# An attention-and-MLP block: another order of work for the first group of 512 rows

## The chip, the cores and the metric

The kernel runs on one core of a Trainium2 chip. The metric is the device time of one execution in microseconds (us), lower is better. A core has TensorE (PE, with its weight loads shown apart as PEld), VectorE (DVE), ScalarE (ACT), GpSimd (POOL) and SyncE (SP), which here issues nearly all transfers. Each engine works through its own instructions in order.

## The reference

```python
mod = (silu(c) @ w_mod)                       # c: 1x448, w_mod: 448x2688 -> six rows of 448
sa, ca, ga, sb, cb, gb = six rows of mod
h = layernorm(x) * (1 + ca) + sa              # x: 2048 x 448
q, k, v = split(h @ wqkv)                     # 16 heads of 28
scores = q @ k.T * 28 ** -0.5                 # key at most 255 rows back, causal
x = x + ga * ((softmax(scores) @ v) @ wo)
h = layernorm(x) * (1 + cb) + sb
x = x + gb * (mish(h @ w1 + b1) @ w2)         # w1: 448x1792, w2: 1792x448
```

All of it is float32. The kernel reaches that precision with two-part numbers: a value is split into `hi` (rounded to fp32r) and `lo` (the rest), and a product is the sum of `hi*hi`, `hi*lo` and `lo*hi`.

## The kernel before, in words

The 2048 rows are worked through in four groups (`NG`) of 512 (`GT`). For each group the normalised rows are transposed in four chunks `ci` of 128 features (the last one holds 64 features twice, for `hi` and `lo`), scaled and shifted by the modulation columns `cols`, and split into `hh` and `hl`. Then `wqkv` is applied in eleven matmuls a tile (`passes`). The tiles 0 to 6 hold 128 columns each of q and k: 0 to 3 reach over q, and 3 (its second half) to 6 over k. The tiles `v0` to `v3` hold V for 128 rows each.

q and k go out through `qk_out`: ACT copies `hi`, DVE forms `lo`, and `put` stores both to a scratch tensor `scr` in HBM. `L(i)` loads head i's q and k back from there, with features and parts on 84 partitions. The function waits on SP until the stores that it reads have landed.

For a head i, `A(i, t)` multiplies q and k for 128 rows, and DVE takes the maxima of the rows (line 580); `M2` transposes the maxima of two heads and sends them by DMA into rows 84 and 85 of the q tile, so that `B(u)` gets the scores with the maxima already subtracted. ACT takes the exponential twice (`P` and `Ph`), POOL forms the rest `Pl`, and `PV` multiplies both with V. `A` runs `LEAD` = 3 heads ahead of `B`.

Between these steps PE gets other work from generators. `fill_main(g)` yields the projections that are still missing, then the transposes and projections of the next group; a credit that grows by `RATE[g]` per step says how many. `fill_side(g)` yields small jobs: the norm of the next group, the modulation of `wo` and others. `pipe` delays the copies behind a tile by a step each, and `later` holds transfers that are issued one at a time or all at once by `flush`. `need(keys, g)` flushes and runs fillers until the given tiles are stored; `load_slot(i)` calls it and then `L(i)`.

The first group has an order of its own, written out by hand (lines 365 to 406):

- SP issues `cT`, x of group 0 (two pieces), the four pieces of `w_mod`, twenty of `wqkv`, then x of group 1.
- DVE takes the statistics of the four row tiles, then sums `w_mod` weighted by `sT` into `acc01` (`mod_sum`, line 145 and 147).
- POOL takes one reciprocal root for all four tiles (lines 206, 207) and the negated mean (211, 212); ACT normalises tile by tile (218).
- PE transposes each tile (376) and then multiplies `acc01` with ones, one column at a time (`mod_cols`, 152), so that the modulation stands on partitions; `mod_cols_out` copies it to `cols`.
- ACT forms `hh` (239), DVE `y` in place (236) and `hl` (243).
- ACT and POOL split the first 384 columns of the weights, ACT, DVE and POOL the other two blocks (164, 170, 172).
- PE does the tiles 0, 3 and 4 together in three rounds (`first`, line 401); all three are then copied and stored.
- POOL builds the mask, `fdf`, the constant columns of V and the rows of -1 in the six K tiles (lines 412 to 433).
- Fillers run until all V tiles are done; five heads are loaded; then `A` runs for three heads with fillers between.

Of the kernel before, what the change touches and what calls it, by code (L numbers as in the profile page):

```python
# [18 lines left out]
EPS = 1e-5  # L19
# [32 lines left out]
def adaln_block(ctx: ExitStack, tc: tile.TileContext, x, wqkv, wo, w1, b1, w2, c, w_mod, out):  # L52
# [19 lines left out]
    vp, vp_s = pool("vp")  # L72
    st0, st0_s = pool("st0")
# [3 lines left out]

    ACT.add_instruction(mybir.InstLoadActFuncSet(
# [18 lines left out]
    cT = cst.tile([112, 4], F32, name="cT")  # L97
# [35 lines left out]
    cols = cst.tile([128, 4, 4], F32, name="cols")  # L133

# [63 lines left out]
    def gen_ln(tiles, pl, xn_tiles, key, act=False, mv=None):  # L198
# [10 lines left out]
        if act:  # L209
            nm = pl.tile([128, 4], F32, name=f"nm{key}")  # L210
            POOL.tensor_tensor(nm, mv[:, :, 0], rs, op=ALU.mult)
            POOL.tensor_scalar(nm, nm, -1.0, None, op0=ALU.mult)
        yield
        xs = xn_tiles()
        for t in range(4):
            xn = xs[t]
            if act:
                ACT.activation(xn[:, 0:D], tiles[t], AF.Identity, scale=rs[:, t:t + 1], bias=nm[:, t:t + 1])
# [8 lines left out]
        if not act:  # L227
            dup(xs[3])
# [12 lines left out]
    def hT_lo(p, ci, hh, hl, si):  # L241
        hT_y(p, ci, si)
        DVE.tensor_tensor(hl[:, ci], p, hh[:, ci].bitcast(F32), op=ALU.subtract)
# [9 lines left out]
    def gen_ln1(g, act=False):  # L253
        def xn_tiles():
            return [xin[g][:, t] for t in range(4)]
        for r in gen_ln([xin[g][:, t, 0:D] for t in range(4)], qk, xn_tiles, f"a{g}", act):
            if r:
                XS[g] = r
            yield "dve"
# [42 lines left out]
    later = []  # L302

# [4 lines left out]
    def qk_out(g, m, p, st=None):  # L308
        st = st or qk.tile([128, 2, GT], F32R, name=f"st{g}_{m}", tag="qs", bufs=3)
# [11 lines left out]

        def put():
            for a, b, pa, ph in ((0, qn, 0, 2), (qn, 128, 1, 0)):
                if a < b:
                    dma(scr[r0 + a:r0 + b, pa:pa + 2, gs], st[a:b].bitcast(F32))
                    dma(scr[r0 + a:r0 + b, ph, gs], st[a:b, 0].bitcast(F32))
# [39 lines left out]
    ln0 = gen_ln1(0, True)  # L366
    for _ in range(5):
        next(ln0)
    for k in range(4):
        mod_sum(k, wm01[k], acc01)  # L370
    pm = bank("sA", 2, "mc01")
    trs = [bank(("sB", "mm")[ci // 2], 2, f"tr0{ci}") for ci in range(4)]
    for t in range(4):
        next(ln0)
        for ci in range(4):
            PE.transpose(trs[ci][:, t * 128:(t + 1) * 128], XS[0][t][:, ci * 128:(ci + 1) * 128], ident)
# [13 lines left out]
    x_load(1)  # L390
    for c0, c1 in QCOLS[1:]:
        for ci in range(4):
            split_hi(wqs[ci][:, c0:c1], wq3[:, ci, c0:c1], ACT)
    for (c0, c1), eng in zip(QCOLS[1:], (DVE, POOL)):
        for ci in range(4):
            split_lo(wqs[ci][:, c0:c1], wq3[:, ci, c0:c1], wql[:, min(ci, 2), c0:c1], ci, eng)
    first = [(m, bank(tag, b, f"qk0_{m}"), qk_passes(0, m)) for m, tag, b in ((0, "pv", 1), (3, "tr", 1), (4, "sA", 2))]
    for lo_n, hi_n in ((0, 3), (3, 6), (6, 11)):
        for m, p, ps in first:
            for n in range(lo_n, hi_n):  # L400
                PE.matmul(p, ps[n][1], ps[n][0], start=(n == 0), stop=(n == 10))
    for m, p, ps in first:
        st = st0.tile([128, 2, GT], F32R, name="st0_4") if m == 4 else None
        for f in qk_out(0, m, p, st):
            f()
        flush()
    st0_s.close()
    att, att_s = pool("att")

    identr = att.tile([128, 128], BF16, name="identr")  # L410
    mask = att.tile([128, 384], F32, name="mask")
    POOL.memset(mask, 0.0)
    POOL.affine_select(mask, mask, pattern=[[1, 384]], compare_op=ALU.is_ge, fill=NEG, base=-1,
                       channel_multiplier=-1)
    POOL.affine_select(mask, mask, pattern=[[-1, 384]], compare_op=ALU.is_ge, fill=NEG, base=W,
                       channel_multiplier=1)
    fdf = att.tile([128, 512], F32, name="fdf", tag="P", bufs=3)
# [4 lines left out]
                       fill=-2.0 ** 100, base=0, channel_multiplier=-1)  # L422
    fdmask = att.tile([128, 256], BF16, name="fdmask")
    for v in V:
        POOL.memset(v[:, :, 28:29].bitcast(F32), 1.0)
        POOL.memset(v[:, :, 29:32].bitcast(F32), 0.0)
    Q2 = [att.tile([86, 2, GT], F32R, name=f"q2_{i}") for i in range(NQ // 2)]
    Q3 = [Q2[i // 2][:, i % 2] for i in range(NQ)]
    K3 = []
    for i in range(NK):  # L430
        t = att.tile([86, GT + W], F32R, name=f"k3_{i}")
        POOL.memset(t[64:86, :].bitcast(F32), -1.0)
        K3.append(t)
# [404 lines left out]
    def fill_main(g):  # L838
        if g == 0:
            yield from gen_qkv(0, VT + (1, 5, 2, 6))  # L840
# [34 lines left out]
    RATE = {0: 0.48, 1: 0.91, 2: 0.91, 3: 0.65}  # L875
# [8 lines left out]
    def need(keys, g):  # L884
        flush()
# [184 lines left out]
```

## Time and profile before

| | us |
|---|---|
| median of 3 runs | 734.92 (732.76 to 738.67) |
| profiled execution | 735.41 |
| its span, first to last instruction | 733.6 |
| PE busy | 692.8 (94%) |
| ACT, DVE, POOL busy | 392.0, 383.1, 326.5 |
| DMA | 83.86 MB, 114 GB/s over the span |

In the rows below a time is a microsecond of the span. In a row of the order of time, the first number is the start and the second the length; `x4` is a count, and the bracket tells how long the engine had been idle and what ended that. A line number is that of the kernel before.

### The profile page before, as it was taken

How to read it: one execution, taken by the hardware profiler on the slowest of the kernel's cores; microseconds unless marked ns; L12 is line 12 of the kernel's file. 1: busy time of each engine (PE TensorE's matmuls, PEld its weight loads, DVE VectorE, ACT ScalarE, POOL GpSimd, SP SyncE). 2: the span in 40 equal slices, each digit the busy share in tenths (PEclk: the TensorE clock that was granted, in tenths of full speed). 3: DMA queues.
4: the chain of work that ended last, by engine and by line, in shares of the span. 5: the costliest groups of instructions: out<-in, count | busy, mean ns of one | idle time of the engine just before them, and what ended most of it. 6: DMA issues, size and time to landing. Idle time of an engine off the chain costs nothing.

```text
span 733.6 us, 11903 instructions
## 1 busy us (share of the span) xinstructions
PE 692.8 (94%) x3969; PEld 589.6 (80%) x3969; DVE 383.1 (52%) x1014; ACT 392.0 (53%) x740; POOL 326.5 (45%) x358
## 2 busy tenths in 40 slices
PE   3987989999999999999999899999999999999996
PEld 3765767888889888888887678878888888888885
DVE  4858645587865688665667943342324132413113
ACT  3516767776776677767878974343223223322221
POOL 4624788676766586766778953523010000000000
PEclk9999999999999999999999999999999999999999
DMA  8675554365384364462566174400200020001001
GB/s 213 185 249 190 179 158 140 92 204 157 95 263 134 97 205 136 146 197 75 170 206 195 46 239 141 137 13 1 101 0 1 1 100 1 1 0 51 1 0 51
DMA packets 48121, 83.86 MB, mean 114 GB/s; under 512 B 6126, under 2 KB 26108, under 8 KB 48060
## 3 DMA queue, kind: packets, MB, share of 16 engines
q1 hardware_dynamic: 48060, 83.10, 37.5%
q8 instruction: 32, 0.52, 0.3%
q14 instruction: 29, 0.24, 0.1%
HBM read 53.45 MB, written 29.36 MB: 113 GB/s over the span
## 4 chain that ended last, share of the span: by engine, by line
PE 75%; DVE 9%; DMA 6%; ACT 4%; SPq 2%; issue 2%; POOL 1%; DVEq 0%; POOLq 0%; ACTq 0%
PE z L814 20%; PE pv L640 8%; PE qk L294 7%; PE acc L992 6%; PE acc L993 6%; PE acc L991 6%; PE sA L578 5%; PE wo L294 4%; PE sB L608 4%; PE qk_v L294 3%; PE sB L619 3%; DVE junk L580 3%; SPq L59 2%; PE et L651 1%; ACT P L622 1%
## 5 line engine op out<-in xcount | busy, mean ns | idle before, releaser
L630 POOL TENSOR_TENSOR Pl<-P,Ph 128x512 fp32r<-128x512 f32 (+2 forms) x192 | 232.9, 1221 | 84.4 <-ACT Ph L623 50.9
L580 DVE CUSTOM_DVE_ANT_0 junk<-sA,mask 128x384 f32<-128x384 f32 (+2 forms) x256 | 135.3, 529 | 105.2 <-PE sA L578 99.8
L622 ACT ACTIVATE P<-sB 128x512 f32<-128x512 f32 (+2 forms) x192 | 109.8, 572 | 67.7 <-PE sB L619 62.2
L822 DVE TENSOR_TENSOR al<-t,ah 128x512 fp32r<-128x512 f32 x56 | 38.8, 692 | 205.1 <-ACT ah L821 205.1
L820 ACT ACTIVATE t<-z,b1c 128x512 f32<-128x512 f32 x56 | 38.6, 689 | 193.2 <-PE z L814 182.2
L578 PE MATMUL sA<-k,q 84*128 84x384 f32 (+2 forms) x256 | 100.8, 397 | 9.7 <-DVE mx L580 5.4
L623 ACT ACTIVATE Ph<-sB 128x512 fp32r<-128x512 f32 (+2 forms) x192 | 109.3, 569 | 0.0
L814 PE MATMUL z<-hhf,w 128*128 128x512 f32 x224 | 89.4, 399 | 0.0
L814 PE MATMUL z<-hlf,w 128*128 128x512 f32 x224 | 88.8, 396 | 0.0
L991 PE MATMUL acc<-w2h,ah 128*128 128x448 f32 x224 | 82.2, 367 | 0.0
L992 PE MATMUL acc<-w2l,ah 128*128 128x448 f32 x224 | 82.0, 366 | 0.0
L993 PE MATMUL acc<-w2h,al 128*128 128x448 f32 x224 | 81.9, 366 | 0.0
L640 PE MATMUL pv<-Ph,v 128*60 128x256 f32 (+2 forms) x352 | 76.8, 292 | 2.2 <-ACT o L645 2.1
L640 PE MATMUL pv<-Pl,v 128*60 128x256 f32 (+2 forms) x352 | 74.1, 285 | 3.1 <-POOL Pl L630 3.0
L608 PE MATMUL sB<-q,k 86*128 86x256 f32 (+1 forms) x352 | 74.7, 286 | 1.3 <-DMA q<-mr 1.2
L814 PE MATMUL z<-hhf,w1l 128*128 128x512 f32 x168 | 66.3, 395 | 0.0
L608 PEld LDWEIGHTS sB<-q,k 86*128 86x128 f32 x352 | 61.7, 190 | 3.3 <-DMA q<-mr 1.5
L578 PEld LDWEIGHTS sA<-k,q 84*128 84x128 f32 x256 | 49.0, 193 | 18.0 <-DVE mx L580 11.5
L619 PE MATMUL sB<-fdmask,identr 128*128 128x128 bf16 (+1 forms) x320 | 60.3, 254 | 0.0
L640 PEld LDWEIGHTS pv<-Ph,v 128*60 128x60 f32 x352 | 45.6, 133 | 16.6 <-ACT o L645 4.3
L640 PEld LDWEIGHTS pv<-Pl,v 128*60 128x60 f32 x352 | 45.0, 132 | 13.2 <-POOL Pl L630 6.3
L645 ACT ACTIVATE o<-pv 60x512 f32<-60x512 f32 x64 | 37.8, 591 | 24.0 <-PE pv L640 23.2
(149 smaller groups left out, 1257.9 us busy)
## 6 DMA issues: line engine op xcount, KB each, us to landing
scr<-st SPq DMA_DIRECT2D x24, 512.0 KB
k<-scr SPq DMA_DIRECT2D x48, 252.0 KB
q<-scr SPq DMA_DIRECT2D x64, 168.0 KB
scr<-st SPq DMA_DIRECT2D x32, 256.0 KB
x<-x1d SPq DMA_DIRECT2D x10, 448.0 KB
xin<-in_A_x_dram SPq DMA_DIRECT2D x8, 448.0 KB
xr<-in_A_x_dram SPq DMA_DIRECT2D x16, 224.0 KB
x1d<-xr SPq DMA_DIRECT2D x16, 224.0 KB
```

The lines of the kernel that those rows point to most:

```text
L294: PE.matmul(p, b, a, start=(n == 0), stop=(n == 10))
L578: PE.matmul(p[:, c0:384], q[0:84, t * 128:(t + 1) * 128], k[0:84, t * 128 + c0:t * 128 + 384], start=True, stop=True)
L580: DVE.tensor_tensor_reduce(out=junk[:, c0:384], in0=p[:, c0:384], in1=mask[:, c0:384], scale=1.0, scalar=-3.0e38, op0=ALU.add, op1=ALU.max ...
L608: PE.matmul(p[:, c:c + 128 * (t1 - t0)], k[:, jj * 128:(jj + 1) * 128], q[:, t0 * 128:t1 * 128], start=(n == 0), stop=False, skip_group_ch ...
L622: ACT.activation(P[:, c0:], p[:, c0:], AF.Exp, scale=SCALE)
L623: ACT.activation(Ph[u][:, c0:], p[:, c0:], AF.Exp, scale=SCALE)
L630: eng.tensor_tensor(Pl[u][:, a:b], Pt[u][:, a:b], Ph[u][:, a:b].bitcast(F32), op=ALU.subtract)
L640: PE.matmul(pv[0:60, t0 * 128:t1 * 128], V[j % NV][:, h, :], P[u][:, c:c + 128 * (t1 - t0)], start=(P is Ph and b == 0 and n == 0), stop=F ...
L814: PE.matmul(zb[n], ps[m][1], ps[m][0], start=(m == 0), stop=(m == 10))
L991: PE.matmul(p, ah[n][:, ts], w2h[f], start=(f == 0), stop=False)
L992: PE.matmul(p, ah[n][:, ts], w2l[f], start=False, stop=False)
L993: PE.matmul(p, al[n][:, ts], w2h[f], start=False, stop=(f == NF - 1))
```

## The change

- `cT` is loaded through ACT's queue, ahead of ACT's table load. The last piece of `w_mod` comes in two transfers and is summed in two halves.
- The first norm takes its reciprocal roots for two tiles at a time; the negated mean is one DVE operation for two tiles.
- Dummy transposes of the identity (`warm`) stand on PE: 46 before the first real one, 2 after each row tile (4 after the last), 12 after the modulation columns.
- ACT forms `y` for the odd chunks in place of DVE. The weight splits of chunks 2 and 3 stand between the `hh`.
- POOL fills five of the six K tiles and the mask at the start; the V constants and `fdf` follow the first weight splits.
- PE does the tiles 0 and 3 first. Their stores that heads 0 and 1 need go out first, then L(0) and L(1), then the rest; then tile 4. The V block's weights are split by DVE (two) and POOL (two), the third block's likewise.
- After L(2) and L(3), nine filler steps run (v0, v1, tile 1), then `A` for three heads with a filler step after each of the twelve (before: one step after every second); L(4) follows the second head. Tile 6 is left for the main loop.
- In the main loop `RATE[0]` is 0.56 in place of 0.48, side steps of group 0 start two steps earlier, and `need` returns at once, without a flush, when its tiles are out.
- All fillers of group 0 take their PSUM banks from the tag `mm`.

```diff
+    cT = cst.tile([112, 4], F32, name="cT")
+    nc.scalar.dma_start(cT, c.rearrange("o (k p) -> p (o k)", p=112))
     ACT.add_instruction(mybir.InstLoadActFuncSet(
...
-    dma(cT, c.rearrange("o (k p) -> p (o k)", p=112))
     x_load(0)
...
-        dma(t, w_mod[k * 112:(k + 1) * 112, 0:2 * D])
+        for s in (slice(0, 2 * D),) if k < 3 else (slice(0, D), slice(D, 2 * D)):
+            dma(t[:, s], w_mod[k * 112:(k + 1) * 112, s])
...
+    def k3_tile(pl, i):
+        t = pl.tile([86, GT + W], F32R, name=f"k3_{i}")
+        POOL.memset(t[64:86, :].bitcast(F32), -1.0)
+        K3.append(t)
+    for i in range(NK - 1):
+        k3_tile(kq, i)
+    mask = kq.tile([128, 384], F32, name="mask")
...
+    for t in range(4):
+        ln_stats(xs0[t][:, 0:D], mv0[:, t, :], qk, f"a0{t}")
+        if t % 2:
+            h = slice(t - 1, t + 1)
+            POOL.tensor_scalar(rs0[:, 0, h], mv0[:, h, 1], EPS, None, op0=ALU.add)
+            POOL.tensor_tensor(rs0[:, 0, h], rs0[:, 0, h], mhalf[:, h], op=ALU.pow)
+    def nm0(t):
+        h = slice(t, t + 2)
+        DVE.scalar_tensor_tensor(rs0[:, 1, h], mv0[:, h, 0], -1.0, rs0[:, 0, h], op0=ALU.mult, op1=ALU.mult)
...
+    for k in range(3):
+        if k < 2:
+            nm0(2 * k)
         mod_sum(k, wm01[k], acc01)
+    for s in (slice(0, D), slice(D, 2 * D)):
+        mod_sum(3, wm01[3][:, s], acc01[:, s])
+    def warm(n):
+        for _ in range(n):
+            PE.transpose(wb[:, 0:128], ident, ident)
+    warm(46)
...
     for t in range(4):
-        next(ln0)
+        norm0(t)
         for ci in range(4):
             PE.transpose(trs[ci][:, t * 128:(t + 1) * 128], XS[0][t][:, ci * 128:(ci + 1) * 128], ident)
+        warm(2 + 2 * (t == 3))
     for i in range(2):
         mod_cols(acc01[:, i * D:(i + 1) * D], pm[:, 4 * i:4 * i + 4])
+    warm(12)
...
+    first_split(0)
+    first_split(1)
...
     for ci in range(4):
         hT_hi(trs[ci], ci, hh, 0)
-        hT_lo(trs[ci], ci, hh, hl, 0)
+        if ci % 2:
+            first_split(2 + ci // 2)
+            ACT.activation(trs[ci], trs[ci], AF.Identity, scale=cols[:, 1, ci:ci + 1], bias=cols[:, 0, ci:ci + 1])
+        hT_lo(trs[ci], ci, hh, hl, 0, ci % 2 == 0)
...
+    x_load(1)
+    split_cols(*QCOLS[1], (DVE, DVE, None, None))
+    first_tiles([(0, bank("pv", 1, "qk0_0")), (3, bank("tr", 1, "qk0_3"))])
+    for m in (0, 3):
+        PARTS[0, m].pop(0)()
+    PARTS[0, 0].pop(0)()
+    L(0)
+    L(1)
+    flush()
+    split_cols(*QCOLS[1], (None, None, POOL, POOL))
+    first_tiles([(4, bank("sA", 2, "qk0_4"))])
+    flush()
+    split_cols(*QCOLS[2], (POOL, POOL, DVE, DVE))
     st0_s.close()
...
-            yield from gen_qkv(0, VT + (1, 5, 2, 6))
+            yield from gen_qkv(0, VT[:2] + (1,) + VT[2:] + (5, 2, 6))
...
-    RATE = {0: 0.48, 1: 0.91, 2: 0.91, 3: 0.65}
+    RATE = {0: 0.56, 1: 0.91, 2: 0.91, 3: 0.65}
...
     def need(keys, g):
+        if all((g, m) in done for m in keys):
+            return
         flush()
...
-    for i in range(LEAD + 1):
+    for i in range(2, LEAD + 1):
         load_slot(i)
-    need({f"v{t}" for t in range(4)}, 0)
-    load_slot(LEAD + 1)
+    for _ in range(9):
+        fill0()
...
     for i in range(LEAD):
         for t in range(4):
             A(i, t)
-            if t % 2:
-                pipe.step()
-                next(fillers[0])
-                flush()
+            fill0()
             side_step(0, False)
         if i % 2:
-            pipe.step()
-            next(fillers[0])
             M2(i // 2)
+            load_slot(LEAD + 1)
...
-            if v > 1:
+            if v > 1 or g == 0:
                 side_step(g, k == 1 and a < NS)
```

More of the change, by code (lines that the diff above doesn't have):

```diff
@@ L226, in gen_ln @@
             yield xs
-        if not act:
-            dup(xs[3])
+        dup(xs[3])
     def tr_chunk(xs, ci, p):
@@ L251, in adaln_block, with gen_ln1 @@
     XS, HT = {}, {}
-    def gen_ln1(g, act=False):
+    def gen_ln1(g):
         def xn_tiles():
             return [xin[g][:, t] for t in range(4)]
-        for r in gen_ln([xin[g][:, t, 0:D] for t in range(4)], qk, xn_tiles, f"a{g}", act):
+        for r in gen_ln([xin[g][:, t, 0:D] for t in range(4)], qk, xn_tiles, f"a{g}"):
             if r:
@@ L320, in store, with rows @@
             later.append(put)
+        def rows(a, b, pa, ph):
+            if a < b:
+                dma(scr[r0 + a:r0 + b, pa:pa + 2, gs], st[a:b].bitcast(F32))
+                dma(scr[r0 + a:r0 + b, ph, gs], st[a:b, 0].bitcast(F32))
+        parts = [lambda: rows(qn, 128, 1, 0), lambda: rows(0, qn, 0, 2)]
         def put():
[L323 to L326, printed above, removed]
+            while parts:
+                parts.pop(0)()
             done.add((g, m))
+        PARTS[g, m] = parts
         return hi, lo, store
@@ L388, in adaln_block @@
         hT_hi(trs[ci], ci, hh, 0)
-        hT_lo(trs[ci], ci, hh, hl, 0)
[L390 to L405, printed above, removed]
-        flush()
[L407 to L417, printed above, removed]
+        if ci % 2:
+            first_split(2 + ci // 2)
+            ACT.activation(trs[ci], trs[ci], AF.Identity, scale=cols[:, 1, ci:ci + 1], bias=cols[:, 0, ci:ci + 1])
+        hT_lo(trs[ci], ci, hh, hl, 0, ci % 2 == 0)
+    for v in V:
+        POOL.memset(v[:, :, 28:29].bitcast(F32), 1.0)
+        POOL.memset(v[:, :, 29:32].bitcast(F32), 0.0)
+    fdf = kq.tile([128, 256], F32, name="fdf")
     POOL.memset(fdf[:, 0:256], 0.0)
@@ L422, in adaln_block, with L, split_cols, first_tiles @@
                        fill=-2.0 ** 100, base=0, channel_multiplier=-1)
+    Q2 = [kq.tile([86, 2, GT], F32R, name="q2_0")]
+    def L(i):
+        g, h = divmod(i, H)
+        q, k = Q2[i % NQ // 2][:, i % 2], K3[i % NK]
+        f0, f1 = h * DH, D + h * DH
+        q0, k0 = g * GT, max(g * GT - W, 0)
+        l0 = k0 - (g * GT - W)
+        dma(q[0:84, :].bitcast(F32), scr[f0:f0 + DH, :, q0:q0 + GT].rearrange("d a n -> (d a) n"))
+        dma(k[0:84, l0:].bitcast(F32), scr[f1:f1 + DH, :, k0:q0 + GT].rearrange("d a n -> (d a) n"))
+    def split_cols(c0, c1, engs):
+        for ci in range(4):
+            if engs[ci]:
+                split_hi(wqs[ci][:, c0:c1], wq3[:, ci, c0:c1], ACT)
+        for ci in range(4):
+            if engs[ci]:
+                split_lo(wqs[ci][:, c0:c1], wq3[:, ci, c0:c1], wql[:, min(ci, 2), c0:c1], ci, engs[ci])
+    def first_tiles(tiles):
+        for lo_n, hi_n in ((0, 3), (3, 6), (6, 11)):
+            for m, p in tiles:
+                ps = qk_passes(0, m)
+                for n in range(lo_n, hi_n):
+                    PE.matmul(p, ps[n][1], ps[n][0], start=(n == 0), stop=(n == 10))
+        for m, p in tiles:
+            for f in qk_out(0, m, p):
+                f()
+    x_load(1)
[11 more added lines that the diff above has]
+    split_cols(*QCOLS[2], (POOL, POOL, DVE, DVE))
+    st0_s.close()
+    att, att_s = pool("att")
+    identr = att.tile([128, 128], BF16, name="identr")
     fdmask = att.tile([128, 256], BF16, name="fdmask")
[L424 to L427, printed above, removed]
+    Q2 += [att.tile([86, 2, GT], F32R, name=f"q2_{i}") for i in range(1, NQ // 2)]
     Q3 = [Q2[i // 2][:, i % 2] for i in range(NQ)]
[L429 to L433, printed above, removed]
+    k3_tile(att, NK - 1)
     O2 = []
@@ L900, in load_slot, with fill0 @@
         L(i)
-    for i in range(LEAD + 1):
+    def fill0():
+        pipe.step()
+        next(fillers[0])
+        flush()
+    for i in range(2, LEAD + 1):
         load_slot(i)
-    need({f"v{t}" for t in range(4)}, 0)
-    load_slot(LEAD + 1)
+    for _ in range(9):
+        fill0()
     DVE.tensor_copy(identr, ident)
-    DVE.tensor_copy(fdmask, fdf[:, 0:256])
+    DVE.tensor_copy(fdmask, fdf)
     for i in range(LEAD):
@@ L973, in adaln_block @@
             PV(u - 2, Ph)
[L974 removed]
+    for st in (FW["s2"], att_s, kq_s, vp_s):
         st.close()
```

62 lines of the change are left out of this document (27 added, 35 removed).

## The prediction

> **What bounds the kernel now.** I read the kernel first by stages: busy time of each engine in stretches, cut where the work changes. The columns are the stretch, its length, then busy us (and instructions) of PE, PEld, DVE, ACT, POOL, the granted clock, the DMA share and GB/s.
>
> ```profile
> 0.00:19.49 19.49, 6.97 (x33) 6.45 (x33) 8.48 (x23) 7.13 (x12) 8.36 (x19) 1.00 0.82 216
> 19.49:29.80 10.31, 9.95 (x34) 7.50 (x35) 10.17 (x11) 7.31 (x13) 5.72 (x4) 1.00 0.68 193
> 29.80:44.86 15.06, 14.36 (x67) 12.22 (x66) 6.47 (x12) 3.98 (x7) 9.01 (x34) 1.00 0.73 214
> 44.86:58.28 13.42, 10.83 (x39) 7.21 (x40) 11.31 (x41) 1.76 (x3) 2.22 (x6) 0.87 0.57 192
> 58.28:137.60 79.32, 71.73 (x469) 57.87 (x470) 49.83 (x176) 58.43 (x134) 58.77 (x61) 0.98 0.55 165
> 137.60:440.00 302.40, 293.01 (x1994) 251.76 (x1994) 209.89 (x618) 224.00 (x435) 211.93 (x196) 1.00 0.52 158
> ```
>
> From 137.60 on PE is busy 97% of the time and the order of work there hardly changes, so that part is only shifted. Everything this change can win lies before 137.60: 12.5 us of idle PE ahead of the first projection, 0.7 between 29.80 and 44.86, 2.6 in the stretch in which the first maxima are taken, 7.6 in group 0's attention.
>
> The second view is the order of time up to the first projection, where the chain runs through DMA, DVE, PE and ACT in turn.
>
> ```profile
> 10.09 2.72 ACT L218 ACTIVATE xin<-xin,nma,rsa 128x448 f32<-128x448 f32 x4 [7.07 <-POOL nma L212]
> ...
> 10.90 4.03 PE L376 MATMUL tr<-ident,xin 128*128 128x128 f32 x16 [10.90 <-ACT xin L218]
> ...
> 13.09 1.15 DVE L147 SCALAR_TENSOR_TENSOR acc<-wm,sT,acc 112x896 f32<-112x896 f32 x1 [0.48 <-DMA wm<-in_w_mod_dram]
> ...
> 14.73 3.25 PE L152 MATMUL mc<-ones,acc 112*128 112x1 f32 x16
> ...
> 18.66 2.79 ACT L239 ACTIVATE hh<-tr,cols 128x512 fp32r<-128x512 f32 x4 [1.72 <-DVE cols L157]
> ...
> 19.49 0.79 PE L401 MATMUL qk<-hh,wq 128*128 128x512 f32 x1 [1.52 <-ACT hh L239]
> ```
>
> The modulation columns set the start: the last `w_mod` piece lands at 13.09, its sum ends at 14.24, sixteen one-column matmuls run to 17.98, `hh` follows at 18.66.
>
> The third view is the clock. I cut the span into pieces of 3.41 us, because the records change speed on that grid.
>
> ```profile
> 10.50:13.91 3.41, 2.91 (x13) 2.51 (x14) 2.60 (x3) 2.77 (x5) 1.85 (x4) 1.00 1.03 248
> 20.74:24.15 3.41, 3.08 (x7) 2.49 (x8) 3.34 (x6) 3.41 (x8) 0.20 (x1) 1.00 1.04 270
> 24.15:27.56 3.41, 3.41 (x16) 2.73 (x15) 3.38 (x4) 1.45 (x3) 3.41 (x3) 1.00 0.63 222
> 48.04:51.46 3.42, 1.98 (x8) 1.09 (x9) 2.87 (x11) 0.60 (x1) 0.85 (x2) 1.00 0.30 116
> 51.46:54.87 3.41, 3.41 (x10) 2.43 (x10) 2.91 (x8) 0.00 (x0) 1.13 (x4) 0.50 0.92 317
> 54.87:58.28 3.41, 2.48 (x13) 1.57 (x12) 2.78 (x12) 1.16 (x2) 0.24 (x1) 1.00 0.13 45
> 92.41:95.82 3.41, 1.34 (x10) 1.18 (x11) 0.77 (x4) 0.26 (x1) 3.41 (x4) 1.00 0.81 176
> ```
>
> Same matmuls, 7 in one piece and 15 or 16 in the next: 0.43 us against 0.23 apiece. So PE ran at half speed until 24.15 (the clock column, 1.00 there, doesn't show it) and full speed followed a piece with 3.08 us of matmuls. A piece with 1.98 us of work was followed by one at 0.50; one with 2.48 was not. Each half-speed piece costs about 3.41/2 = 1.7 us.
>
> **The change part by part.**
>
> *Head of the kernel.* `cT` goes to ACT's queue, so x and `w_mod` are issued one slot earlier.
>
> ```profile
> 0.73 0.39 SPq L59 DMA_DIRECT2D cT<-in_c_dram  x1
> ...
> 4.51 0.63 DVE L192 BATCH_NORM_STATS2 sta<-xin 128x6 f32<-128x448 f32 x1 [0.87 <-DMA xin<-in_A_x_dram]
> ...
> 8.09 0.23 POOL L206 TENSOR_SCALAR rsa<-mva 128x4 f32<-128x4 f32 x1 [6.64 <-DVE mva L193]
> ...
> 8.40 1.04 POOL L207 TENSOR_TENSOR rsa<-rsa,mhalf 128x4 f32<-128x4 f32 x1
> ```
>
> With gaps that is 0.45 us. The issue that ACT gains, about 0.4 as on SP, delays only its table load and Exp, whose result DVE now takes after the statistics. The extra issue for the split last `w_mod` piece takes the slot back for the weights behind it. POOL's five K memsets and the mask move to the front:
>
> ```profile
> 29.81 0.42 POOL L412 MEMSET mask<- 128x384 f32 x1
> ...
> 31.78 0.31 POOL L418 MEMSET fdf<- 128x256 f32 x1
> ...
> 33.96 4.15 POOL L432 MEMSET k<- 22x768 f32 x6
> ```
>
> 5 x 4.15/6 = 3.5 plus 31.78 - 29.81 = 2.0. They lie in the 6.64 us in which POOL waits for statistics, but not wholly: begun near 1.45 they end near 6.9, and two tiles' statistics are there near 5.7 (4.06 and twice 0.63 with an aggregate behind each). That cover is short by 1.3 us, and I count it. Reciprocal root of the first half 6.9 + 0.23 + 1.04 = 8.2; the negated mean, now one small DVE operation, 8.5; ACT at 0.68 a tile does tiles 0 and 1 by 9.9, 2 and 3 by 11.3 (before: 12.81). Transposes end near 12.0 if PE is free. The last `w_mod` piece lands at 12.6; its second half needs half of 1.15, so the sum is ready at 13.3, not 14.24.
>
> *The warming transposes*: 46 + 10 + 12 = 68 on PE, in its queue ahead of real work. Their price depends on the clock:
>
> ```profile
> 1.00 0.29 POOL masks.py:199 TENSOR_SCALAR_AFFINE_SELECT ident<-ident 128x128 f32<-128x128 f32 x1
> ...
> 12.75 1.78 PEld L376 LDWEIGHTS tr<-ident,xin 128*128 128x128 f32 x9 [0.49 <-POOL xin L196]
> ...
> 57.08 0.60 PE L232 MATMUL tr<-ident,xin 128*128 128x128 f32 x4
> ```
>
> (4.03 - 0.49)/16 = 0.22 each at half speed, the gap taken off; 0.60/4 = 0.15 at full speed with the tail of the last in it, so I take half of 0.22, 0.11. The identity is there at 1.3. 46 at 0.22 last to 11.4, two us past the first normalised tiles. If the clock rises after one or two grid pieces (16 to 32 of them at 0.22), they end between 8 and 10, on time.
>
> Do transposes raise it? In 10.50:13.91 thirteen transposes made PE 2.91 us busy, near the 3.08 that sufficed later, and the sixteen one-column matmuls behind them still took 0.20 each, which is half speed:
>
> ```profile
> 225.54 0.77 PE mc L152 x8
> ```
>
> is 0.10 each. That speaks against. For it: 54.87:58.28 kept the clock with 2.48 us, of which 0.60 were those four transposes; without them it has 1.88, less than the 1.98 that lost it. A solid train of 46 is denser than anything transposed here. I take it that they do, at about 0.7 against 0.3. The Trainium skill ("TensorE: Matmul & The Clock Gate", Part 4: PE-mode transpose) says that transpose mode doesn't count as PE-busy the same way and that the full clock "doesn't engage" for it; transposes run at both speeds here (0.22 and 0.60/4), while 10.50:13.91 agrees with the page. By that rule the sum would be the first rival's.
>
> *Start of the projections, clock up.* Columns: 13.3, eight remaining matmuls at 0.10, 14.2, then the 0.7 that lay between 17.98 and 18.66: `hh` at 14.9, first matmul near 15.7 instead of 19.49. ACT now holds two weight splits and two of the affine passes between the `hh`:
>
> ```profile
> 13.45 1.69 ACT L164 ACTIVATE wq<-wqs 128x384 fp32r<-128x384 f32 x3 [0.64 <-DMA wqs<-in_A_wqkv_dram]
> 14.06 2.95 POOL L170 TENSOR_TENSOR wql<-wqs,wq 128x384 fp32r<-128x384 f32 x3 [0.95 <-DMA wqs<-in_A_wqkv_dram]
> ...
> 20.32 0.69 DVE L243 TENSOR_TENSOR hl<-tr,hh 128x512 fp32r<-128x512 f32 x1
> ```
>
> Four `hh` and two passes at 0.7, two splits at 0.56: 14.9 + 5.3 = 20.2, and DVE's last `hl` at 21.0. Tile 0's last pass waits for it, tile 3's five follow at 0.23: 22.4. Tile 4's eleven: 24.9. The same 33 matmuls ended at 29.8. **-4.9 us** (3.8 from the start; 2 of slow clock less new waits for `hl`).
>
> *Tiles among the maxima.* Before, 88 matmuls and twelve score tiles filled 29.8 to 58.28, where the first exponentiated scores begin. Now 33 matmuls come first (nine steps: 24.9 + 7.1 = 32.0), then 44 with the twelve score tiles: 44 x 0.22 + 12 x 0.25 = 12.7 on PE. DVE needs its 11.3 of the old stretch and about 2 for more `lo` parts: 13.3. I take 15 with waits. The scores need their loads first.
>
> ```profile
> 25.29 4.95 DVE L170 TENSOR_TENSOR wql<-wqs,wq 128x448 fp32r<-128x448 f32 x3
> ...
> 30.27 0.62 DVE L172 TENSOR_TENSOR wq<-wqs,wq 64x448 fp32r<-64x448 f32 x1
> ...
> 31.64 6.71 SPq L59 DMA_DIRECT2D scr<-st  x8
> ...
> 44.89 0.47 PE L578 MATMUL sA<-k,q 84*128 84x128 f32 x2 [0.72 <-DMA k<-scr]
> ```
>
> DVE now does two V splits ahead of the first two `lo`: from 21.0 at 0.62 each, or at 4.95/3 = 1.65 if POOL is in its way, so the last `lo` ends near 23.8 or 25.8 (the old ones stood behind three of 1.65 and ended past 31.6). Four stores and four loads then go to SP ahead of everything else. Eight and eight took 44.89 - 31.64 = 13.25; half the bytes, half of that. First scores between 23.8 + 6.6 = 30.4 and 25.8 + 13.25 = 39.0; PE arrives at 32.0. I take 33, nearer the half: so much fewer bytes stand in front. While SP waits in L(0) for stores to land, tile 4's stores, L(2), L(3) and tile 1's stores stand behind it; PE needs L(2) eight score tiles later, some 10 us. V's other two splits and two of the third block's go to POOL, 2.95/3 = 1.0 each at 384 columns, with DVE and POOL otherwise idle; they must be done by the third pass group of the first V tile near 26, or PE waits a few tenths. 33 + 15 = 48 against 58.28: **-10.3 us**, the -4.9 included. Owed at that point: tile 6 (11 x 0.23) and group 1's first four transposes of 57.08, **+3.2**.
>
> *Group 0's attention.* The filler rate 0.56 for 0.48 carries tile 6. A row each for the one long wait:
>
> ```profile
> 88.38 0.44 SPq L59 DMA_DIRECT2D k<-scr  x1
> ...
> 94.48 0.30 PE L578 MATMUL sA<-k,q 84*128 84x128 f32 x1 [3.05 <-DMA k<-scr]
> ```
>
> A load took 6 us and PE stood 3.05, with a half-speed piece (1.7) after it, the one behind 92.41:95.82. `need` now returns without flushing when the tiles are out, so this load no longer has the waiting stores and `wo` pieces put ahead of it. Between nothing and 4.75 of it goes; the owed 3.2 may vanish in the 7.6 of idle PE or cost in full. I count the owed in full and half of the 3.05: **-1.5**. The sum: -10.3 + 3.2 - 1.5 = -8.6.
>
> **The rivals.** (1) *The transposes leave the clock low*, so the warming doesn't warm. All of them at 0.22: 46 to 11.4, 26 more to 17.1, columns (3.25) to 20.4, twelve more to 23.0, first matmul 3.5 us later than before. Ten matmuls at 0.43 to 27.3, twelve at 0.23 to 30.1, tile 4 to 32.6; with 7.1 and 15, 54.7. -3.6 + 3.2 - 1.5 = -1.9: 733, with 729 to 739 by the same bounds. For it speaks 10.50:13.91, and that page; against it 54.87:58.28.
>
> (2) *The early loads stall* (slower). Place: SP in L(0). At 39.0 PE has stood 6 us and loses a half-speed piece: -8.6 + 6 + 1.7 = -0.9; L(2), held behind the same wait and tile 4's stores, then comes late by another 3 or so: 737.5. It is slower than before once the two waits pass 7 us together, that is with the first load past about 38. For it: the 13.25 us of 31.64 to 44.89, and 6 us for one load at 88.38. Against: half the bytes.
>
> (3) *Better than counted*: the owed work lies wholly in idle time and the wait at 91 goes: -10.3 - 4.75 = -15; I count it as the forecast's low tail.
>
> **How the numbers follow.** The profiled execution took 735.41 us, 1.8 around its span of 733.6, and 0.5 above the median of 734.92. 735.41 - 8.6 - 0.5 = 726.3; I say 726.5. Chances: forecast 0.57, low clock 0.31, stalled loads 0.12. The forecast's own range is 721 to 732. Leaving out the ends of the low-clock case beyond 736, most of the stalled case and the far tail of (3), the range is 720.5 to 736. About 1% (7.35 us) is what a measurement of this kernel can tell from no change: 727.6 and 742.3. Two thirds of the forecast and a tenth of the low-clock case lie under 727.6: 0.41. Above 742.3 lies half of the stalled case (its waits with a low clock beside them) and the far end of the low-clock case: 0.08. The rest, 0.51, is within 1%.
>
> **What would show it.** The first projection starts near 15.7 and its matmuls are 0.23 apart (low clock: near 23 and 0.43); tile 4's last at 25; first score tile near 33, with a wait for `k<-scr` under 2 us; first exponentiated scores near 48; no half-speed piece between 48 and 58; group 0's end near 129; from there the same 300 us to 440's counterpart. The forecast is wrong if PE's transposes still come 0.22 apart past 9 us, if the first score tile waits for its load past 38, or if group 0's attention grows by over 4 us.

## The result and the profile after

| | median, us | lowest to highest | runs |
|---|---|---|---|
| before | 735.60 | 732.76 to 739.34 | 15 |
| changed | 728.66 | 726.01 to 734.85 | 15 |

The ratio is 0.9903, 95% interval 0.9883 to 0.9922: the change saves 6.9 us, where 8.6 was forecast. The profiled execution of the changed kernel took 734.85 us, the longest of its fifteen, with a mean granted clock of 0.985; a second profile of the same kernel (`again` below, 727.71 us, clock 0.993) lies near the median, so both are shown.

First the stages, cut at the same events as before: first projection, end of the tiles 0, 3 and 4, first score tile, half a microsecond ahead of the first exponentiated scores, start of group 1, third activation of the MLP. The changed kernel:

```profile
0.00:18.35 18.35, 15.10 (x100) 14.31 (x100) 8.68 (x26) 6.08 (x10) 11.91 (x25) 0.91 0.78 211
18.35:27.32 8.97, 8.12 (x34) 6.19 (x35) 6.84 (x10) 7.18 (x13) 5.23 (x26) 1.00 0.92 259
27.32:36.35 9.03, 7.39 (x35) 5.96 (x33) 4.77 (x7) 4.11 (x8) 5.87 (x6) 1.00 0.71 212
36.35:49.58 13.23, 12.68 (x58) 9.89 (x58) 11.98 (x42) 1.83 (x4) 2.23 (x6) 1.00 0.64 209
49.58:131.78 82.20, 76.80 (x485) 62.55 (x484) 50.48 (x178) 59.90 (x136) 58.96 (x61) 0.94 0.55 173
131.78:439.46 307.68, 296.01 (x1994) 254.68 (x1994) 209.80 (x618) 224.05 (x435) 212.04 (x196) 0.99 0.52 157
```

The same kernel in the profile `again`:

```profile
0.00:16.25 16.25, 13.99 (x101) 12.97 (x101) 8.57 (x26) 6.09 (x10) 11.65 (x25) 1.00 0.79 221
16.25:25.21 8.96, 8.11 (x33) 6.16 (x34) 6.84 (x10) 7.18 (x13) 5.22 (x27) 1.00 0.93 266
25.21:34.30 9.09, 7.43 (x35) 5.96 (x33) 4.76 (x7) 4.16 (x8) 5.87 (x6) 1.00 0.72 228
34.30:47.53 13.23, 12.66 (x58) 9.88 (x58) 11.98 (x42) 1.78 (x4) 2.23 (x6) 1.00 0.65 215
47.53:127.10 79.57, 74.05 (x486) 60.17 (x484) 50.27 (x178) 59.69 (x136) 58.91 (x61) 0.98 0.56 178
127.10:432.29 305.19, 294.24 (x1994) 253.07 (x1994) 210.15 (x618) 224.00 (x435) 212.15 (x196) 0.99 0.52 159
```

Read downwards against the stages before, `again` is 10.75 us ahead when the exponentiated scores begin (47.53 against 58.28) and still 10.50 ahead at group 1's start (127.10 against 137.60). At the third activation of the MLP only 7.70 are left (432.29 against 439.99): the last stretch, which does the same 1994 matmuls, takes 305.19 instead of 302.40. Behind that point both kernels need 293.6 us (725.9 - 432.29, 733.6 - 439.99). The first profile lost more there, 307.68, and ends only 0.5 us ahead of the kernel before (733.1 against 733.6). So two questions stand: what the parts of the head and the order were worth, and who took 2.8 us back in a stretch whose order of work the diff changes only through the early return of `need`.

The order of time at the start, TensorE and the sums of `w_mod` on VectorE. The changed kernel:

```profile
1.35 6.96 PE L412 MATMUL warm<-ident 128*128 128x128 f32 x46 [1.35 <-POOL ident masks.py:199]
9.79 0.66 PE L420 MATMUL tr<-ident,xin 128*128 128x128 f32 x4 [1.48 <-ACT xin L391]
...
11.45 2.47 DVE L161 SCALAR_TENSOR_TENSOR acc<-wm,sT,acc 112x896 f32<-112x896 f32 x3 [0.24 <-DMA wm<-in_w_mod_dram]
...
14.72 2.12 PE L166 MATMUL mc<-ones,acc 112*128 112x1 f32 x16
...
18.35 0.50 PE L478 MATMUL qk<-hh,wq 128*128 128x512 f32 x1
```

and `again`:

```profile
1.35 7.26 PE L412 MATMUL warm<-ident 128*128 128x128 f32 x46 [1.35 <-POOL ident masks.py:199]
9.24 0.66 PE L420 MATMUL tr<-ident,xin 128*128 128x128 f32 x4 [0.64 <-ACT xin L391]
...
10.80 2.47 DVE L161 SCALAR_TENSOR_TENSOR acc<-wm,sT,acc 112x896 f32<-112x896 f32 x3 [0.30 <-DMA wm<-in_w_mod_dram]
...
12.73 2.00 PE L166 MATMUL mc<-ones,acc 112*128 112x1 f32 x16
...
16.25 0.50 PE L478 MATMUL qk<-hh,wq 128*128 128x512 f32 x1
```

The head does what the forecast said, and in one of the two profiles it is 2.1 us later. The pieces of the clock's grid say why (changed kernel, columns as in the prediction):

```profile
1.69:5.10 3.41, 3.41 (x19) 3.41 (x18) 0.14 (x1) 0.81 (x1) 3.35 (x6) 1.00 0.78 211
5.10:8.51 3.41, 3.21 (x30) 2.97 (x28) 2.93 (x10) 0.20 (x1) 2.33 (x6) 1.00 1.06 312
8.51:11.93 3.42, 1.77 (x13) 1.52 (x14) 2.84 (x7) 2.72 (x4) 2.48 (x6) 0.97 1.05 258
11.93:15.34 3.41, 3.41 (x20) 3.41 (x18) 1.96 (x3) 1.05 (x2) 2.21 (x3) 0.53 0.64 176
...
66.53:69.94 3.41, 1.36 (x10) 0.97 (x9) 3.34 (x10) 2.59 (x6) 2.43 (x3) 0.98 0.09 7
69.94:73.35 3.41, 3.35 (x12) 2.68 (x13) 2.87 (x10) 0.54 (x2) 1.05 (x1) 0.50 0.77 211
...
428.40:431.81 3.41, 1.21 (x10) 0.92 (x9) 1.06 (x3) 2.98 (x6) 0.54 (x1) 0.97 1.04 316
431.81:435.22 3.41, 3.41 (x12) 3.04 (x11) 0.69 (x1) 0.60 (x1) 3.27 (x5) 0.53 0.94 344
```

Nineteen transposes touch the first full piece, thirty the next, and TensorE did nothing else until then: transposes alone raised the clock (the clock column, 1.00 in both pieces, doesn't show it). If each took 0.22 or 0.11 us, (6.96 - 46 x 0.11)/0.11 = 17 of the 46 ran at 0.22 and the others at 0.11. Then TensorE waited 1.48 us for the first normalised tile, the piece held 1.77 us of work, and the clock was taken back for the one behind it. In `again` the first tile came at 9.24, the wait was 0.64, and the clock stayed; there the wait also lay across the border of two pieces with 3.08 and 2.90 us of work, so the length of the wait and its place on the grid aren't told apart. The same pattern (1.36, then 0.50; 1.21, then 0.53) returns in group 0 and at the start of the MLP.

### The profile page after: what moved, and what is told of

The parts are those of the page before. It is cut to its first block, busy times and chain, and to the rows that moved or that the text cites. A ratio compares the mean times of both kernels' runs of the same rounds, so it can differ in the third digit from the quotient of the medians.

```text
span 733.1 us, 12035 instructions
## 1 busy us (share of the span) xinstructions
PE 702.1 (96%) x4037; PEld 600.1 (82%) x4037; DVE 379.5 (52%) x1015; ACT 392.4 (54%) x742; POOL 326.8 (45%) x358
## 4 chain that ended last, share of the span: by engine, by line
PE 77%; DVE 7%; ACT 5%; issue 2%; DMA 2%; POOL 1%; SPq 0%; DVEq 0%; ACTq 0%; POOLq 0%
PE z L875 20%; PE pv L701 8%; PE qk L299 8%; PE acc L1056 6%; PE acc L1055 6%; PE acc L1057 6%; PE sA L639 5%; PE sB L669 4%; PE wo L299 4%; PE qk_v L299 4%; PE sB L680 3%; DVE junk L641 2%; ACT P L683 2%; PE et L712 2%; ACT Ph L684 1%
## 5 line engine op out<-in xcount | busy, mean ns | idle before, releaser
L701 PE MATMUL pv<-Ph,v 128*60 128x256 f32 (+2 forms) x352 | 78.3, 297 | 2.8 <-ACT o L706 2.6
```

The source lines that it names most:

```text
L701: PE.matmul(pv[0:60, t0 * 128:t1 * 128], V[j % NV][:, h, :], P[u][:, c:c + 128 * (t1 - t0)], start=(P is Ph and b == 0 and n == 0), stop=F ...
```

## The experiments

The table collects them. Ratios are to the kernel before, timed on the same chip in the same session; the last three columns come from each kernel's own profile: start of the first exponentiated scores, of group 1's first, and of the MLP's third activation.

| kernel | median, us | ratio, 95% interval | scores | group 1 | MLP 3rd |
|---|---|---|---|---|---|
| before | | | 58.86 | 138.10 | 439.99 |
| `again` | 729.43 | 0.9923 (0.9898 to 0.9947) | 48.11 | 127.60 | 432.28 |
| `nowarm` | 729.54 | 0.9929 (0.9905 to 0.9954) | 52.97 | 131.84 | 434.99 |
| `headonly` | 732.44 | 0.9967 (0.9949 to 0.9985) | 52.70 | 130.14 | 436.59 |
| `flush` | 733.11 | 0.9966 (0.9937 to 0.9994) | 48.39 | 129.67 | 437.15 |
| `again2` | 729.36 | 0.9916 (0.9892 to 0.9939) | 48.61 | 129.61 | 432.67 |
| `banks` | 725.73 | 0.9867 (0.9841 to 0.9893) | 48.72 | 126.97 | 430.57 |
| `nowarmtr` | 731.17 | 0.9939 (0.9914 to 0.9963) | 51.31 | 133.81 | 436.90 |
| `bankslong` | 726.81 | 0.9881 (0.9855 to 0.9908) | 49.11 | 127.84 | 432.09 |
| `banks2` | 725.32 | 0.9873 (0.9845 to 0.9902) | 48.58 | 126.42 | 428.33 |
| `headbanks` | 730.08 | 0.9931 (0.9904 to 0.9957) | 52.75 | 131.00 | 433.78 |
| `oldhead` | 731.74 | 0.9947 (0.9926 to 0.9968) | 54.62 | 132.01 | 434.88 |

The first four ran in one session, the next four in a second, the last three in a third.

**`again`, `again2`: the changed kernel unedited.**

> The changed kernel once more, for a second profile. By my account its profile differs from run to run in how many pieces of 3.41 us run at half speed: the profile shown has four after the first projection (1.7 us each, near 8 with the one in the head), and the median has fewer. Expected: 0.988 to 0.992 of before, and in this profile at most three such pieces. Rival: the pieces are part of the change (always four, same places), and the median gain comes from elsewhere.

> The changed kernel once more, nothing edited, beside the next three. Both theories: 0.992 of before, as the first repeat had (0.9923). In its trace the fourth-last group's first four transposes of the output (line 236, near 422-428 us) wait about 2.2 us again, and the two first rectified-tile activations (line 881) after the second stand 10.7 us apart.

Both gave the first result again, as good as within its interval (0.9923 lies a hair above its upper end, 0.9922). The number of half-speed pieces does differ from run to run: up to 440 us the granted clock falls to about a half in six pieces of the first profile (from 11.8, 59.6, 69.8, 73.2, 418.0 and 431.6) and in two of `again` (from 67.0 and 425.4). `again2` shows the 2.20 us wait at the MLP but no half-speed piece behind it, and 9.11 us instead of 10.67 from the second to the third activation.

**`nowarm`: no warming transposes.**

```diff
-    wb = bank("tr", 1, "warm")
...
-    warm(46)
...
-        warm(2 + 2 * (t == 3))
...
-    warm(12)
```

> All 68 dummy transposes left out, the rest as changed. Theory A (the warming pays): PE is at half speed in the head and for the first ten projections, 10 x 0.20 = 2 us, and the columns take 0.20 each: 2 to 4 us slower than the changed kernel, 0.994 to 0.996 of before. Theory B (the transposes stand in the way of what they speed up): the columns are no longer queued behind them, the first projection starts near 17 instead of 18.35, and this gives back the 2 us: within 1 us of the changed kernel.

The time is that of `again`, and yet the head is slower. TensorE without warming:

```profile
9.21 3.68 PE L418 MATMUL tr<-ident,xin 128*128 128x128 f32 x16 [9.21 <-ACT xin L391]
12.68 3.26 PE L166 MATMUL mc<-ones,acc 112*128 112x1 f32 x16
17.46 0.80 PE L474 MATMUL qk<-hh,wq 128*128 128x512 f32 x1 [1.52 <-ACT hh L243]
18.05 0.63 PE L474 MATMUL qk<-hh,wql 128*128 128x512 f32 x1
```

Columns at 0.20 us each, the first projection at 17.46 and the next 0.6 behind it: half speed. The scores begin 4.9 us later than in `again`, group 1 4.2 later, the MLP's third activation only 2.7 later, and the end no later by the medians. So Theory B's number came true, but not its reason: the warming is worth something at the start, and something that goes out with it gives part of it back behind. A part of that can be named: the profiles with warming spend 10.7 us from the second to the third activation of the MLP (the changed kernel, `again`, `headonly` and `flush`), this one 7.58 and the kernel before 7.65. `nowarm` keeps only 1.5 of these 3.1 us by its profile, since it has a half-speed piece of its own shortly before (416.8 to 420.2).

**`headonly`: the new head with the old order.** Behind the head, the old code: the tiles 0, 3 and 4 together, fillers until V is done, five heads loaded at once, a filler step after every second score tile, `VT + (1, 5, 2, 6)`, rate 0.48, `need` always sending the stores. A part of the edit:

```diff
-            yield from gen_qkv(0, VT[:2] + (1,) + VT[2:] + (5, 2, 6))
+            yield from gen_qkv(0, VT + (1, 5, 2, 6))
...
-    for i in range(2, LEAD + 1):
+    for i in range(LEAD + 1):
         load_slot(i)
-    for _ in range(9):
-        fill0()
+    need({f"v{t}" for t in range(4)}, 0)
```

> The new head up to the first weight splits, and behind it the order of before (three tiles at once, five loads after all V tiles, maxima after that, RATE 0.48, need as before). By the profiles the head brings 29.8 - 27.3 = 2.5 us and the order the rest: 0.996 to 0.997. Rival 1: the head brings nearly all (0.990 to 0.992). Rival 2: the head brings nothing, since group 0 waits for other things anyway (0.999 to 1.001).

The head alone starts the scores 6.2 us earlier, so the new order adds 4.6 to that in `again`. But the median fell by 2.4 us only, as foreseen, and for another reason than foreseen: the head brought more than 2.5 us, and at the MLP this kernel too had lost time (8.0 ahead at group 1, 3.4 at the third activation, a half-speed piece near 391 us in it).

**`flush`: `need` always sends the waiting stores first.**

```diff
     def need(keys, g):
-        if all((g, m) in done for m in keys):
-            return
         flush()
```

> As changed, but need always flushes the waiting transfers first, as before. My theory: the wait of 3.05 us for k near 91 comes back, with a half-speed piece behind it: 3 to 4.7 us slower than the changed kernel, 0.994 to 0.997 of before. Rival: the wait went because the work around it moved, and the flush is worth nothing: within 1 us of the changed kernel.

Two waits of TensorE for a k tile appear in group 0 that `again` doesn't have (order of time of `flush`):

```profile
85.07 0.30 PE L639 MATMUL sA<-k,q 84*128 84x128 f32 x1 [1.51 <-DMA k<-scr]
...
115.19 0.41 PE L639 MATMUL sA<-k,q 84*128 84x384 f32 x1 [1.66 <-DMA k<-scr]
```

Together 3.2 us. In `again` the only wait for k is that of the first score tile (its table of waits up to 140 us):

```profile
PE sA L639 <- DMA k<-scr: 0.5, 1, 0.5
```

From the scores to group 1 `flush` takes 81.3 us and `again` 79.5, so in the profiles the early return in `need` earns its term of 1.5. The waits came back at other places than near 91. The times say less: by the ratios `flush` is 0.4% (3.2 us) slower, the intervals overlap, and its twelve runs spread the widest, from 726.75 to 738.18.

**Who takes the 2.8 us: `banks`, `nowarmtr`.** The rows at the start of the MLP, TensorE, ScalarE and VectorE. Before:

```profile
432.14 0.59 PE L651 MATMUL et<-ident,o 124*128 124x124 f32 x4
432.56 0.60 PE L232 MATMUL ot<-ident,on 128*128 128x128 f32 x4
...
432.34 0.69 ACT L820 ACTIVATE t<-z,b1c 128x512 f32<-128x512 f32 x1 [0.67 <-PE z L814]
...
439.99 0.69 ACT L820 ACTIVATE t<-z,b1c 128x512 f32<-128x512 f32 x1 [1.96 <-PE z L814]
```

`again`:

```profile
421.41 0.59 PE L712 MATMUL et<-ident,o 124*128 124x124 f32 x4
424.20 0.63 PE L236 MATMUL ot<-ident,on 128*128 128x128 f32 x4 [2.20 <-ACT w L178]
...
421.61 0.69 ACT L881 ACTIVATE t<-z,b1c 128x512 f32<-128x512 f32 x1 [0.66 <-PE z L875]
...
432.28 0.69 ACT L881 ACTIVATE t<-z,b1c 128x512 f32<-128x512 f32 x1 [1.90 <-PE z L875]
...
423.71 0.34 DVE L726 TENSOR_TENSOR ol<-ol,et 128x224 f32<-128x224 f32 x1
```

Before, the output transposes `ot` ran right behind the last head pair's `et`. In `again` they wait 2.20 us. The row names ScalarE, but the last reader of `et` is the VectorE addition that ends at 424.05, and `ot` starts at 424.20: `ot` waits for the PSUM bank in which `et` lies. `et` has the tag `tr` of the attention's PSUM pool; that pool is closed and the MLP's opened in its place, and `ot` is the first to ask that one for a bank. The kernel before asked its pool first for `sA`. The changed kernel asks first for `tr`, since its line 407, `wb = bank("tr", 1, "warm")`, takes a bank for the warming (a line of the whole diff that isn't among those shown above). If places go by the order of asking, `ot` now gets `et`'s bank. One edit moves only the asking:

```diff
-    wb = bank("tr", 1, "warm")
...
-    warm(46)
     pm = bank("sA", 2, "mc01")
     trs = [bank(("sB", "mm")[ci // 2], 2, f"tr0{ci}") for ci in range(4)]
+    wb = bank("tr", 1, "warm")
+    warm(46)
```

> Only the order in which PSUM banks are first asked for is changed: the warming transposes' bank is asked for behind the banks of the tags sA, sB and mm, not ahead of all; every instruction of the head stays. Theory of the bank: asked for first, the tag tr lies at the front of the pool, and the pool of the MLP, opened in the same place, gives that bank to the last group's output transposes, which then wait until VectorE has read the last head pair out of it: 2.2 us of wait, and then a piece at half speed, 10.7 us instead of 7.6 between the second and third activation of the MLP. So the wait goes, and the time falls by 3.0 us against the changed kernel: 0.988 of before, about 726.4 us. Rival, the phase: the 3 us hang on when the MLP begins and on where a half-speed piece falls; then nothing changes, 0.992, and the 10.7 us stay.

> The changed kernel with the warming transposes' bank asked for behind the others, a second time, as the base for the next two: 0.9867 of before again, within 0.003. In the trace no wait ahead of the last group's first output transposes, and group 0's first exponentiated scores near 48.5 us.

The other edit takes all warming out and keeps the first line of it:

```diff
     wb = bank("tr", 1, "warm")
...
-    warm(46)
...
-        warm(2 + 2 * (t == 3))
...
-    warm(12)
```

> All 68 warming transposes out, as in the kernel without warming, but the bank for them is still asked for first (and never used). Theory of the bank: the 3.0 us at the start of the MLP come back without any warming: 0.997 of before, about 732.5 us, against 0.993 (729.5) of the kernel without warming and without that bank. Rival, the phase: 0.993 as that kernel.

With the bank asked for later the wait is gone (`banks2`):

```profile
420.26 0.59 PE L712 MATMUL et<-ident,o 124*128 124x124 f32 x4
420.69 0.60 PE L236 MATMUL ot<-ident,on 128*128 128x128 f32 x4
```

and with no warming but the bank asked for first it is there (`nowarmtr`):

```profile
430.38 0.63 PE L236 MATMUL ot<-ident,on 128*128 128x128 f32 x4 [2.20 <-ACT w L178]
```

The wait follows the line that asks for the bank, in both directions: all six profiles of kernels that ask for `tr` first have it, with 2.20 or 2.21 us (the first profile of the changed kernel, `again`, `again2`, `headonly`, `flush`, `nowarmtr`), and none of the seven others has. That the places in the pool go by the order of asking is inferred from this; no view shows the places themselves. From the second to the third activation it is 7.65 us before, 7.58 in `nowarm`, 7.77 and 7.87 in `banks` and `banks2`; 9.11 with the wait alone (`again2`, `nowarmtr`); 10.67 with the wait and a half-speed piece behind it (`again`). So in the profiles it costs 1.5 or 3.0 us. (`bankslong` has 8.67 without this wait; there the third four `ot` wait 1.75 us for `hlo` from VectorE, a wait of 0.7 before.) `banks` is 3.6 us faster than `again2` beside it, and its slowest run (727.86) is faster than the fastest of `again2` (727.99); `banks2` is as much under before as `banks`. The 3.6 are more than the 1.5 or 3.0 of the wait, and the rest isn't placed: the profiles of `banks` and `again2` take about as long from group 1 to the third activation (303.60 and 303.06 by the table), since `banks` has a half-speed piece from 411.8 in that stretch and `again2` has none.

Of `nowarmtr` the trace was foreseen and the time not: 732.5 (0.997) was expected and 731.17 measured, an interval that holds the rival's 0.993 and not 0.997. Without warming, then, the bank's price doesn't show in the times. One difference of the two profiles bears on that. In `nowarmtr` the sixteen columns took 2.24 us (3.26 in `nowarm`) and the first projection started at 16.53 (17.46):

```profile
9.30 3.67 PE L419 MATMUL tr<-ident,xin 128*128 128x128 f32 x16 [9.30 <-ACT xin L391]
12.78 2.24 PE L166 MATMUL mc<-ones,acc 112*128 112x1 f32 x16
```

The transposes of the rows, with the first few columns, had raised the clock without any warming, and it was lost again at 16.7. Equal in bank order, the warming brings 0.9929 - 0.9870 = 0.6% (`nowarm` against the mean of `banks` and `banks2`, intervals apart) or 0.9939 - 0.9916 = 0.2% (`nowarmtr` against `again2`, intervals overlapping).

**`bankslong`: 60 warming transposes, three between the tiles.** The edit against `banks`:

```diff
-    warm(46)
+    warm(60)
...
-        warm(2 + 2 * (t == 3))
+        warm(3 + (t == 3))
```

> The bank order as in the kernel before this one, and 60 warming transposes ahead of the first tile instead of 46, three instead of two between the tiles, so that TensorE isn't idle between 8.3 and 9.8 us. Theory: the clock is then not taken back at 11.8 us in the executions in which it was (first projection at 18.35 us there, at 16.25 where it wasn't), so 0 to 2 us less than with 46, in the middle 1: 0.987 of before, about 725.5 us. Rival: 14 more transposes at 0.11 us end at about 9.9, after the first row tile is ready, and the clock was high in most executions anyway: 0.988 to 0.989, no gain or 0.5 us lost.

No gain: the first projection moved back,

```profile
17.04 0.50 PE L478 MATMUL qk<-hh,wq 128*128 128x512 f32 x1
```

against 16.20 in `banks`. The extra transposes stand ahead of the first tile, and in neither profile had the clock been taken back at the head, so there was nothing to save. The time, 0.9881, is the rival's.

**Head and order, added up: `headbanks`, `oldhead`.** `headbanks` is `headonly` with the edit of `banks`. `oldhead` has the new order behind an old head (`cT` on SP ahead of x, one root for four tiles, the last piece of `w_mod` whole, no warming at all); POOL's early memsets, ACT's `y` for the odd chunks and the new places of the weight splits stay. A part of the edit:

```diff
-    nc.scalar.dma_start(cT, c.rearrange("o (k p) -> p (o k)", p=112))
+    dma(cT, c.rearrange("o (k p) -> p (o k)", p=112))
...
-        for s in (slice(0, 2 * D),) if k < 3 else (slice(0, D), slice(D, 2 * D)):
+        for s in (slice(0, 2 * D),):
...
-        if t % 2:
-            h = slice(t - 1, t + 1)
+        if t == 3:
+            h = slice(0, 4)
...
-    warm(46)
```

> The new head with the old order behind it, with the warming bank asked for behind the others, so that only the head differs from before: what is left out is the reordering of group 0 and the part of the change that lets a wait for keys pass without sending all stores. If the bank cost this kernel 1.5 to 3 us as it cost the changed one, 0.9925 to 0.9945 of before, about 729.5 us in the middle; first exponentiated scores near 52.7 us, 6.2 before the old ones. Rival: the bank's wait was hidden behind the old order; then 0.9967 as without the edit.

> The new order behind the old head: no warming, the vector c loaded first on SP's queue, one root for all four row tiles, the last piece of w_mod and its sum in one. If the two parts add, it saves what the whole saves less what the head saves: at the first exponentiated scores 10.8 - 6.2 = 4.6 us, at group 1's start 10.5 - 8.0 = 2.5 us, so 0.9935 to 0.9965 of before, about 731.5 us, with the first projection at 18.5 to 19.5 us. Rival: the order is worth something only when the head is early, because its second load of x and its early value projections need the time that the head frees: 0.998 to 1.000.

Both fell into their ranges: the head without the bank's wait is worth 5.3 us, the order alone 3.7, and 9.0 together stand against 9.9 measured for the whole without the wait (mean of `banks` and `banks2`: 735.4 - 725.5). Within intervals of about 2 us on each side, they add. By the profiles they don't quite: at group 1's start `oldhead` is 6.1 us ahead of before where 2.5 was expected, and `headbanks` 7.1, together more than the 11.1 and 11.7 of `banks` and `banks2`. The first projection of `oldhead` came later than expected and at half speed:

```profile
20.02 0.79 PE L474 MATMUL qk<-hh,wq 128*128 128x512 f32 x1 [1.52 <-ACT hh L243]
```

The version that beats both kernels is the changed one with the bank asked for later: 725.3 and 725.7 us.

## Why the prediction was right or wrong, point by point

- **The head.** Sum of `w_mod` ready at 13.27 in `again` (forecast 13.3), 13.92 in the first profile, where the first tile and `w_mod` came 0.55 to 0.65 later. The first projection came at 16.25, forecast 15.7. The step that was short: from the sum to the last column 1.46 us passed (13.27 to 14.73), not 0.9. The columns began at 12.73 only, right behind the transposes, which were expected to end near 12.0, and took 2.00/16 = 0.125 us each, not 0.10. The 0.7 behind them held (`hh` at 15.42).
- **Do transposes raise the clock?** Yes, after 17 of them in the one profile and 20 in the other (7.26 us by the same sum), and the 46 ended at 8.3 and 8.6 (forecast 8 to 10). The first rival is out: transposes at 0.22 or more past 9 us, one of the prediction's own signs of being wrong, were seen in the changed kernel only where the clock had been raised and lost again. The Trainium skill ("TensorE: Matmul & The Clock Gate", Part 4: PE-mode transpose) says the full clock doesn't engage for them; x19 against x30 in the two pieces measures the opposite for these float32 transposes, and `nowarmtr` does so once more.
- **The three tiles** were out at 25.21 (forecast 24.9) in `again`, 27.32 in the first profile, where the start was as much later.
- **First score tile** at 34.30, forecast 33: from the end of tile 4 it took 9.1 us, not 8.1. In that time TensorE waits 0.5 us for the first k and, at 30.92, 1.1 of the 1.3 us of this row, until VectorE has formed the `lo` part of a V tile (line 353),

```profile
PE qk L299 <- DVE v L353: 1.3, 2, 1.1
```

 VectorE came to it late, behind its splits of the weights, one of which took 1.67 us at 28.54. With 0.5 us for the first k the second rival, loads stalling past 38, is out. The lead took 13.23 instead of 15. The two errors cancel, which is luck: -10.75 against -10.3, -8.70 in the profile that lost the clock at 11.9.
- **Group 0.** Forecast +3.2 for the owed work and -1.5 for the wait at 91, so +1.7. Measured from 79.32: 79.57 in `again` (+0.25), 77.92 between the same events in `banks2` (-1.4), 82.20 in the first profile (+2.9). The wait for k is gone altogether, where half of it was counted. What the owed work cost stays open: counted in full, 3.2 - 4.75 + 1.7 for the new half-speed piece of `again` (67.0 to 70.4) would be +0.15, near the +0.25; but `banks2`, with one such piece too (58.4 to 61.8), has -1.4. The first profile has three. One stands behind a wait of 1.4 us for a row of maxima (`q<-mr`), the second behind 66.53:69.94, in which VectorE is busy 3.34 of 3.41 us and TensorE waits 1.6 us for its maxima; the third follows the second, though TensorE was busy 3.35 us in it, and no row says why.
- **"From there the same 300 us"**, the argument that the rest is only shifted, is the step that failed: 305.19 and 307.68, not 302.40. The prediction put this stretch at nothing, since the order of work hardly changes. No row of the trace before could show it, but the whole diff could: a new first request in a pool whose places a later pool takes over. The wait and the half-speed piece behind it, 3.0 us together, cover the 2.8 of `again`; the first profile has one more half-speed piece in this stretch (418.0 to 421.4). With that line moved, the same stretch in `banks2` is

```profile
125.92:428.34 302.42, 292.72 (x1994) 251.87 (x1994) 209.76 (x618) 223.92 (x435) 212.18 (x196) 1.00 0.52 158
```

 and with no half-speed piece in it the forecast's mechanism holds to the end. (`banks`, with one, takes 304.10 by the same cut.)
- **The sum.** -8.6 forecast; -6.9 measured with the bank's wait of 1.5 to 3.0 us, -9.9 without. Both lie between 720.5 and 736. That the number came near is in part luck: at group 1's start `again` was 10.5 ahead, 1.9 more than the whole forecast, and then lost the 2.8 that weren't in the sum. The third rival (-15) came true in one of its parts only, the wait at 91.

## What to carry to other kernels

A scratch tile taken at the head of a kernel can move later allocations, even those of a pool opened in its place; when a stretch that the diff hardly touches grows, look for the first instruction there that waits where it didn't, and for who else uses its bank. Judge a warming of the clock by what follows it too: it has to last until the real work arrives, and one gap (1.48 us here) was enough to lose it. And take more than one profile before explaining two microseconds, since two executions of this kernel differed by more than that in where half-speed pieces fell.

## What the runs showed of the hardware

Forty-six 128x128 transposes with nothing else raised the clock: their time apiece fell from 0.22 to 0.11 us after about 3.7 us (17 x 0.22) in one profile and 4.4 (20 x 0.22) in the other. The clock went down after gaps well under the piece: 1.48 us of waiting with 1.77 us of work in the piece (8.51 to 11.93), and 2.20 us of waiting at the MLP with 1.21 of work; the same wait in `again2` and `nowarmtr` didn't cost the clock. The Trainium skill ("TensorE: Matmul & The Clock Gate", Why this matters for your kernels) asks for no idle gaps of more than about 3 us; here half of that was enough when the rest of the piece was sparse. Cut on the grid of each, twelve of the profiles (all but `nowarmtr`, behind 24 us) show 1.21 to 1.97 us of work, once 2.29, in the piece ahead of a loss; pieces with as little as 1.67 us also kept the clock, so the work in a piece doesn't decide alone.

Transposes and one-column matmuls in a row, 9.21 to 15.94 in `nowarm`, filled the records and didn't raise the clock; its piece 10.68:14.09 holds 2.21 us of transposes and 1.41 of columns. In `nowarmtr` the piece 10.00:13.41, with 2.97 us of transposes and 0.64 of columns, was followed by full speed. So the columns may count for less than their records show; which of the two decides wasn't tried.
